# A fused attention and feed-forward kernel: q instead of w_in is loaded in permuted order, and the key-value state is copied across the partition halves

## The chip, the core and the metric

The kernel runs on one core of one Trainium2 chip. The metric is the device time of one execution in microseconds; three runs of the kernel before gave 832.87 in the median (832.84 to 837.14). Five engines work side by side, each through its own instructions in order: TensorE (PE; its weight loads are shown as PEld), VectorE (DVE), ScalarE (ACT), GpSimd (POOL) and SyncE (SP), which here issues nearly all DMAs. The DMAs of a core share 16 DMA engines.

## The reference

Linear attention over 8 batches, 8 heads, 576 tokens, 64 features a head, and then a two-layer feed-forward network on the 4608 rows of 512 that this gives. All numbers are wide: q, k and v are 32-bit floats, the two weight matrices 64-bit floats, which the kernel takes as 64-bit words.

```python
q_s = exp(q - max(q, axis=-1));  q_s = q_s / (sum(q_s, axis=-1) + 1e-9)   # over the 64 features
k_s = exp(k - max(k, axis=2));   k_s = k_s / (sum(k_s, axis=2) + 1e-9)    # over the 576 tokens
kv  = einsum('bhsd,bhse->bhde', k_s, v)                                   # the state: 64 x 64 a head
x   = einsum('bhsd,bhde->bhse', q_s, kv).transpose(0, 2, 1, 3).reshape(4608, 512)
h   = x @ w_in                                                            # 512 x 2048
g   = maximum(h, 0) + log1p(exp(-abs(h)))                                 # softplus
out = g @ w_out                                                           # 2048 x 512
```

## The kernel before

**Tiles.** Two heads make a pair and fill 128 partitions, 64 each; there are 4 pairs (`HP`). The tokens are cut into 9 tiles of 512. The middle dimension of 2048 is cut into 16 weights (`NJ`): weight k holds 128 columns of w_in (as 128 rows of 512 words) and the 128 rows of w_out that go with them.

**State.** For each batch b and pair h, `kv_unit` (L466) takes a tile of keys and values, finds the maxima of the keys, shifts (L516), takes exponentials (L522), multiplies keys and values on TensorE (L527, L532), inverts the sums of the keys (L540, L541) and copies the 64 x 64 state of both heads, scaled, out of PSUM (`keep`, L545) into `kvs[b % 2]`. For b = 0 the maxima come by way of TensorE (L495, L512), which also runs fillers on the identity matrix (L1159).

**q and x.** A q tile holds for 512 tokens the four pairs, 128 partitions x 4 x 512 floats. `q_unit` (L566) takes its softmax: maxima (L576), exchange between neighbouring blocks of 32 partitions (L563), shift (L590), exponential (L593), sums (L596), division (L625), in halves of two pairs. `flip` (L657, for the first tile L680) transposes in blocks of 32. `x_product` (L640, L646) then makes x for two pairs in four quarter products: state and q of one partition half (`zs`), written to one partition half of one of two PSUM banks. The bank is chosen by the partition half z that q and state are read from, and the half of the bank by the pair y within the group of two. So the features of x come out in another order than that of the pairs.

**Where that order is made good.** Before, w_in is loaded with its rows and pieces permuted to that order, by two DMAs of half the partitions each (L286). w_out goes in as it is (L290).

**Weights.** Each weight is turned from 64-bit words into floats and then into a high and a low part: top bits (`top_w`, T, L317), scaling (`scale_w`, M, L309 and L311), sign (`sign_w`, S, L328 and L330), `join_w` (J, L339), and the split into high (P, L350) and low (Q, L352). The first two weights are used unsplit (L708, L758). `up` (U, L720 to L722) and `down` (O, L762 to L764) multiply high x high, low x high and high x low; `softplus` (A, L729) empties the bank of `up`, `split_g` (G, L735 and L738) splits its result. From tile 3 on, two tiles are multiplied together with seven products in place of eight (L847 to L849, L961 to L963), from parts of the weights that were stored to DRAM and are fetched again.

**What sets the order.** The string `ORDER` lists some 3000 steps, and every engine gets its instructions in that order; nothing is reordered later. Around the change it reads `w0.20 b0 b1 q0.0 n k0.0.1 n q0.1 n n ... l0 ... l1 ... l2`: b0 and b1 load the two halves of the first q tile, n loads a tile of keys and values, l a weight, L (as L1) a later q tile by `q_load` (L553). All of these are issued by SP in that order, so a load waits for those ahead of it, and for its buffer. Tiles of keys and values from batch 1 on have two buffers, and GpSimd fills their spare rows (L455) before each load. Weights 10 to 15 are loaded with the tiles of keys and values of batch 1 (`kv_next`, L1044).

Of the kernel before, what the change touches and what calls it, by code (L numbers as in the profile page):

```python
# [15 lines left out]
AF = mybir.ActivationFunctionType  # L16
# [4 lines left out]
B, H, S, D = 8, 8, 576, 64  # L21
DM, DF = 512, 2048
NT = B * S
HP = H // 2
# [13 lines left out]
START = [P * sum(SUBS[:t]) for t in range(len(SUBS) + 1)]  # L38
# [8 lines left out]
TOK = P * max(SUBS)  # L47
# [164 lines left out]
def tile_attn_ffn(  # L212
# [69 lines left out]

    def load_w(k):
        raw[k] = wp.tile([P, 2, DM], I64, name=f"w{k}")
        for y in range(2):
            nc.sync.dma_start(  # L286
                out=raw[k][D * y:D * (y + 1), 0].rearrange("p (g z c) -> p g z c", g=2, z=2),
                in_=w_in[k].rearrange("(z p) (g y c) -> y p g z c", z=2, g=2, y=2)[y],
            )
        nc.sync.dma_start(out=raw[k][:, 1], in_=w_out[k])  # L290

    def words(k, dtype):
# [173 lines left out]
    def kv_unit(b, h, bank):  # L466

        t = loaded.pop((b, h))
        kt, vt = t[:, :, :, 0:D], t[:, :, :, D:KVW if b else 2 * D]
        wide, ps = bank[:, 0:P], (bank[:, 0:D + 1] if b else bank[:, P:P + D])  # L470
        total = ps[:, D:D + 1] if b else banks[h % 2][:, h // 2:h // 2 + 1]
        rest = warm[:, P + D * h:P + D * (h + 1)]
        state = {}

        on_pe = b <= ON_PE

        def top():
            if not b:
                return
            mx = state["mx"] = sm.tile([P, 2, D], F32, name="mx", bufs=3)  # L480
            nc.vector.tensor_reduce(out=mx, in_=kt.rearrange("p c z d -> p z d c"), op=ALU.max, axis=AX.X)  # L481
            if not on_pe:
                mb = state["mb"] = sm.tile([P, 2, D], F32, name="mx", bufs=3)
                nc.gpsimd.partition_all_reduce(  # L484
                    mb.rearrange("p z d -> p (z d)"), mx.rearrange("p z d -> p (z d)"), channels=P,
                    reduce_op=bass_isa.ReduceOp.max,
                )

        def turn():
            if not b:  # L490
                for c in range(NCH, -1, -1):
                    rows = P if c < NCH else TAIL
                    for z in range(2):
                        zs = slice(z * D, (z + 1) * D)
                        nc.tensor.matmul(  # L495
                            bank[zs, c * P:(c + 1) * P] if c < NCH else rest[zs], lhsT=kt[0:rows, c, z],
                            rhs=ident[0:rows, 0:rows], start=True, stop=True,
                        )
                return
            nc.tensor.transpose(wide, state["mx"].rearrange("p z d -> p (z d)"), ident)  # L500

        def across():
            state["m1"] = sm.tile([P, 1], F32, name="m1", bufs=2)
            if not b:
                nc.vector.tensor_reduce(out=state["m1"], in_=rest, op=ALU.max, axis=AX.X)
                nc.vector.tensor_tensor(
                    out=bank[:, 0:1], in0=bank[:, 0:1], in1=state["m1"], op=ALU.max
                )
            nc.vector.tensor_reduce(out=state["m1"], in_=wide if b else bank, op=ALU.max, axis=AX.X)

        def spread():
            nc.tensor.transpose(wide, state["m1"].broadcast_to([P, P]), ident)  # L512

        def shift():
            mb = wide.rearrange("p (z d) -> p z d", z=2) if on_pe else state["mb"]
            nc.vector.tensor_tensor(  # L516
                out=kt, in0=kt, in1=mb.unsqueeze(1).broadcast_to([P, NCH + 1, 2, D]), op=ALU.subtract
            )

        def power():  # L520
            cz = t.rearrange("p c z w -> p (c z) w")[:, :, 0:D]
            nc.scalar.activation(cz, cz, AF.Exp)  # L522

        def product():
            for c in range(0 if b else NCH + 1):
                for z in range(2):
                    nc.tensor.matmul(  # L527
                        total[z * D:(z + 1) * D], lhsT=kt[:, c, z], rhs=one, start=c == 0, stop=c == NCH
                    )
            for c in range(NCH + 1):  # L530
                for z in range(2):
                    nc.tensor.matmul(  # L532
                        ps[z * D:(z + 1) * D], lhsT=kt[:, c, z], rhs=vt[:, c, z], start=c == 0, stop=c == NCH
                    )
            if b == 1:
                kv_next()

        def scale():
            r = sm.tile([P, 1], F32, name="r", bufs=2)
            nc.vector.tensor_scalar(out=r, in0=total, scalar1=EPS, scalar2=W_SCALE, op0=ALU.add, op1=ALU.mult)  # L540
            nc.vector.reciprocal(r, r)  # L541
            state["r"] = r

        def keep():
            nc.scalar.activation(kvs[b % 2][:, h], ps[:, 0:D], AF.Copy, scale=state["r"])  # L545

        none = lambda: None
        return [top] + ([turn, across, spread] if on_pe else [none] * 3) + [shift, power, product, scale, keep]
# [3 lines left out]

    def q_load(t):  # L553
        qt = (wp if t >= SOLO and t % 2 else qp).tile([P, HP * TOK], F32, name="w4" if t >= SOLO and t % 2 else "qt")
        nc.sync.dma_start(out=qt, in_=q[:, HP * START[t]:HP * START[t + 1]])
        qtiles[t] = qt.rearrange("p (h n) -> p h n", h=HP)

    def swapped(m, copy=nc.vector.tensor_copy):

# [497 lines left out]
    with tc.manual_schedule():  # L1057
# [28 lines left out]
        def do(token):  # L1086
# [31 lines left out]
            elif kind == "q":  # L1118
                unit(("q", at[0]), lambda: q_unit(at[0]))[at[1]](*(nc.gpsimd,) * sum(at[2:]))
            elif kind == "x":  # L1120
                t, h, i = at
                unit(("x", t, h), lambda: make_x(t, h))[i]()
            elif kind == "L":
                q_load(at[0])
            elif kind == "D":
                keep_w(at[0])
            elif kind == "R":
                {0: fetch_w, 2: fetch_sums, 3: fetch_in, 4: fetch_in_b}[at[0]](*at[1:])
            elif kind == "Y":
                s, i = at[:2]  # L1130
                unit(("Y", s), lambda: sum_unit(s))[i](*(nc.gpsimd,) * sum(at[2:]))
            elif kind == "y":
                s, i = at[:2]
                unit(("y", s), lambda: sum_out_unit(s))[i](*(nc.gpsimd,) * sum(at[2:]))
            elif kind == "r":
                fetch_block(*at)
            elif kind == "t":
                less_g(*at[:3], *(nc.gpsimd,) * sum(at[3:]))
            elif kind == "e":
                split_right(*at[:4], *(nc.gpsimd,) * sum(at[4:]))  # L1140
            elif kind == "d":
                product_out(*at)
            elif kind == "o":
                unit(("o", at[0]), lambda: end_unit(at[0]))[token.split(".")[1]](*at[1:])
            elif kind == "X":
                p, c, name, *more = token[1:].split(".")
                unit(("X", p, c), lambda: operand_unit(int(p), int(c)))[name](*(nc.gpsimd,) * len(more))
            elif kind == "C":
                p, s, i = at
                unit(("C", p, s), lambda: pair_unit(p, s))[i]()  # L1150
            elif kind == "H":
                split_g(*at[:3], *(nc.gpsimd,) * sum(at[3:]))
            elif kind == "I":
                down(*at)
            elif kind == "F":
                finish(*at)
            elif kind == "w":
                for _ in range(at[1]):
                    nc.tensor.matmul(warm[:, 0:P], lhsT=ident, rhs=ident, start=True, stop=True)  # L1159
            elif kind == "b":  # L1160
                half = slice(2 * at[0], 2 * at[0] + 2)
                nc.sync.dma_start(
                    out=qtiles[0][:, half], in_=q[:, 0:HP * TOK].rearrange("p (h n) -> p h n", h=HP)[:, half]
                )
            elif kind == "n":
                place = dict(engine=nc.vector, queue=nc.scalar) if ahead[0] < HP else {}
                if 2 <= ahead[0] < HP:
                    tag = 2 * ahead[0] - 4 if UNSPLIT < NJ else ahead[0] - 1
                    place |= dict(pool=xp, tag=f"x{tag}", shape=(P, HP * TOK))
                kv_prefetch(**place)  # L1170
            elif kind == "l":
                for k in at:
                    load_w(k)
# [41 lines left out]
```

## Time and profile before

| | |
|---|---|
| median of 3 runs | 832.87 us |
| profiled execution | 832.97 us, span 831.1 us |
| PE busy | 805.5 us (97%), 4312 matmuls |
| PEld busy | 640.8 us (77%) |
| DVE busy | 582.4 us (70%) |
| ACT busy | 484.2 us (58%) |
| POOL busy | 115.1 us (14%) |
| granted TensorE clock, mean | 0.992 of full |
| DMA | 193.72 MB, mean 233 GB/s |
| w_in loads (L286) | 32 of 256 KB, 10.7 us from issue to landing (median) |
| w_out loads (L290) | 16 of 512 KB, 11.6 us |
| q loads | 2 of 512 KB, 4.6 us; 8 of 1024 KB |

Times count from the start of the span. An instruction's row gives its start, how long it took, engine, line, operation, the tile written and the tile read, shapes, and in brackets how long the engine stood idle before it and what ended that. A count (x2) merges neighbours. Matmuls overlap: a row's 0.4 us is longer than the distance to the next. SP's rows are issues, not transfers.

### The profile page before, as it was taken

What the parts mean: (1) busy time and instruction counts of PE and PEld (TensorE: products, weight loads), DVE (VectorE), ACT (ScalarE), POOL (GpSimd) and SP (SyncE); (2) the same over time, 40 slices, a digit from 0 to 9 for tenths busy, and PEclk for the clock granted to TensorE, in tenths of its full rate; (3) what the DMA queues carried; (4) which work ended last, traced back from release to release, by engine and by line L of the source; (5) the groups of instructions that cost most, each with busy time, mean ns of one, the idle gap of its engine ahead of it and who ended that gap; (6) DMA issues with size and microseconds to landing.
All of it is one profiled execution on the core that took longest, in us unless ns stands there. A gap on an engine that the chain in (4) does not pass through costs nothing.

```text
span 831.1 us, 12042 instructions
## 1 busy us (share of the span) xinstructions
PE 805.5 (97%) x4312; PEld 640.8 (77%) x4312; DVE 582.4 (70%) x934; ACT 484.2 (58%) x792; POOL 115.1 (14%) x211
## 2 busy tenths in 40 slices
PE   8898899999999999999999999999999999999997
PEld 7566686888777787788788777888777788888886
DVE  7656895369688886968489889765596852227884
ACT  3687883545554755577786555766574542446652
POOL 1220003101010210101010012250000110700017
PEclk9899999999999999999999999999999999999999
DMA  9999956647689888998696575984766554948845
GB/s 278 247 247 242 246 222 226 206 144 267 233 289 342 273 315 297 323 325 294 227 290 196 164 243 166 314 257 156 226 192 186 183 172 170 271 134 278 253 141 88
DMA packets 120890, 193.72 MB, mean 233 GB/s; under 512 B 8256, under 2 KB 98624, under 8 KB 110592
## 3 DMA queue, kind: packets, MB, share of 16 engines
q1 hardware_dynamic: 117568, 186.67, 70.3%
q0 software_dynamic: 2944, 6.04, 3.6%
q8 instruction: 34, 0.56, 0.3%
q10 hardware_dynamic: 320, 0.26, 0.1%
q14 instruction: 24, 0.20, 0.1%
HBM read 149.95 MB, written 42.99 MB: 232 GB/s over the span
## 4 chain that ended last, share of the span: by engine, by line
PE 81%; DMA 8%; DVE 3%; ACT 2%; POOL 2%; SPq 1%; issue 1%; POOLq 0%; ACTq 0%; DVEq 0%
PE po L847 6%; PE po L849 6%; PE po L848 6%; PE po L963 6%; PE po L961 6%; PE po L962 6%; PE po L762 4%; PE ph L720 4%; PE po L764 4%; PE po L763 4%; PE ph L721 4%; PE ph L722 4%; DMA w<-in_w_in 4%; PE ph L847 3%; PE ph L848 3%; PE ph L849 3%
## 5 line engine op out<-in xcount | busy, mean ns | idle before, releaser
L1006 POOL DMA_DIRECT2D out<-w x92 | 59.4, 653 | 296.9 <-DVE w L998 292.3
L720 PE MATMUL ph<-x,w 128*128 128x512 f32 x164 | 66.3, 404 | 3.5 <-ACT g L729 3.4
L762 PE MATMUL po<-w,g_hi 128*128 128x512 f32 x164 | 65.1, 397 | 2.1 <-ACT g_hi L735 2.1
L721 PE MATMUL ph<-x,w 128*128 128x512 f32 x164 | 64.6, 394 | 0.1
L722 PE MATMUL ph<-x,w 128*128 128x512 f32 x164 | 64.6, 394 | 0.0
L764 PE MATMUL po<-w,g_lo 128*128 128x512 f32 x164 | 64.2, 391 | 0.1
L944 DVE TENSOR_TENSOR g_lo<-w,g_hi 128x512 fp32r<-128x512 f32 x74 | 49.4, 682 | 21.1 <-ACT g_hi L941 21.1
L763 PE MATMUL po<-w,g_hi 128*128 128x512 f32 x164 | 64.0, 390 | 0.0
L941 ACT CAST g_hi<-w 128x512 fp32r<-128x512 f32 x74 | 45.5, 619 | 19.7 <-PE po L962 13.2
L928 DVE TENSOR_TENSOR w<-w,w 128x512 f32<-128x512 f32 x72 | 48.4, 681 | 2.7 <-ACT w L881 1.7
L941 ACT CAST w<-w 128x512 fp32r<-128x512 f32 x52 | 31.8, 620 | 25.7 <-PE po L962 18.9
L870 DVE TENSOR_TENSOR w<-po,w 128x512 f32<-128x512 f32 x24 | 16.5, 686 | 40.8 <-PE po L849 40.8
L738 DVE TENSOR_TENSOR g_lo<-g,g_hi 128x512 fp32r<-128x512 f32 x46 | 31.1, 681 | 19.6 <-ACT g_hi L735 19.5
L729 ACT ACTIVATE g<-ph 128x512 f32<-128x512 f32 x48 | 28.5, 597 | 27.4 <-PE ph L722 27.2
L847 PE MATMUL po<-w,x 128*128 128x512 f32 x112 | 44.3, 395 | 0.0
L849 PE MATMUL po<-w,x 128*128 128x512 f32 x112 | 43.7, 390 | 0.0
L848 PE MATMUL po<-w,x 128*128 128x512 f32 x112 | 43.6, 390 | 0.0
L484 POOL PARTITION_ALL_REDUCE mx<-mx x20 | 20.5, 1027 | 165.8 <-DVE mx L481 145.1
L481 DVE TENSOR_REDUCE mx<-kvt 128x128 f32<-128x640 f32 x28 | 36.8, 1320 | 8.8 <-DMA kvt<-in_kv_tail 6.9
L720 PEld LDWEIGHTS ph<-x,w 128*128 128x128 f32 x164 | 31.2, 190 | 13.1 <-ACT g L729 4.4
L735 ACT CAST g_hi<-g 128x512 fp32r<-128x512 f32 x46 | 28.2, 619 | 21.7 <-PE po L763 15.4
L944 DVE TENSOR_TENSOR w<-w,w 128x512 fp32r<-128x512 f32 x52 | 35.1, 683 | 6.5 <-ACT w L941 6.2
(380 smaller groups left out, 2243.6 us busy)
## 6 DMA issues: line engine op xcount, KB each, us to landing
x<-sums SPq DMA_DIRECT2D x24, 1024.0 KB, 5.6
kvt<-in_kv SPq DMA_DIRECT2D x30, 512.0 KB, 6.8
kept<-w SPq DMA_DIRECT2D x15, 1024.0 KB, 8.2
w<-kept SPq DMA_DIRECT2D x13, 1024.0 KB, 8.3
x<-sums_out SPq DMA_DIRECT2D x44, 256.0 KB, 5.2
w<-kept SPq DMA_DIRECT2D x36, 256.0 KB, 4.6
x<-kept SPq DMA_DIRECT2D x36, 256.0 KB, 4.7
w<-sums_out SPq DMA_DIRECT2D x36, 256.0 KB, 5.7
```

The source lines that it names most:

```text
L720: nc.tensor.matmul(ph, lhsT=w_hi, rhs=x_hi, start=h == 0, stop=False)
L721: nc.tensor.matmul(ph, lhsT=w_lo, rhs=x_hi, start=False, stop=False)
L722: nc.tensor.matmul(ph, lhsT=w_hi, rhs=x_lo, start=False, stop=h == HP - 1)
L762: nc.tensor.matmul(po, lhsT=g_hi[:, ms], rhs=w_hi, start=j == 0, stop=False)
L763: nc.tensor.matmul(po, lhsT=g_hi[:, ms], rhs=w_lo, start=False, stop=False)
L764: nc.tensor.matmul(po, lhsT=g_lo[:, ms], rhs=w_hi, start=False, stop=j == NJ - 1)
L847: nc.tensor.matmul(ph, lhsT=w_hi, rhs=x_hi, start=c == 0 and i in (0, 4), stop=False, **more)
L848: nc.tensor.matmul(ph, lhsT=w_lo, rhs=x_hi, start=False, stop=False, **more)
L849: nc.tensor.matmul(ph, lhsT=w_hi, rhs=x_lo, start=False, stop=c == 1, **more)
L941: nc.scalar.copy(ring[p, i, s][0], right_of(p, i, s))
L944: engine.tensor_tensor(out=lo, in0=right_of(p, i, s), in1=hi.bitcast(F32), op=ALU.subtract)
L1006: nc.gpsimd.dma_start(out=rows(n, c)[:, 32 * a:32 * a + 32].rearrange("(b r) e -> r b e", r=32), in_=flipped(n)[32 * a:32 * a + 32, c].rea ...
```

## The change

The loads of w_in become one DMA of 128 whole rows. A q tile is loaded by four DMAs instead (`q_fetch`): for each group g of two pairs and each partition half z, 64 partitions with 2 pieces of 512 floats. The partition half z of q then holds pair 2g + z, and the pieces y its two heads. The state has to lie the same way, so `keep` copies its two halves separately: head z of pair h goes to the partition half h % 2, place 2 (h // 2) + z. `x_product` stays as it is, and x comes out in the order of the heads.

```diff
     def load_w(k):
         raw[k] = wp.tile([P, 2, DM], I64, name=f"w{k}")
-        for y in range(2):
-            nc.sync.dma_start(
-                out=raw[k][D * y:D * (y + 1), 0].rearrange("p (g z c) -> p g z c", g=2, z=2),
-                in_=w_in[k].rearrange("(z p) (g y c) -> y p g z c", z=2, g=2, y=2)[y],
-            )
+        nc.sync.dma_start(out=raw[k][:, 0], in_=w_in[k])
         nc.sync.dma_start(out=raw[k][:, 1], in_=w_out[k])
...
         def keep():
-            nc.scalar.activation(kvs[b % 2][:, h], ps[:, 0:D], AF.Copy, scale=state["r"])
+            for z in range(2):
+                zs, to = slice(z * D, (z + 1) * D), slice(h % 2 * D, (h % 2 + 1) * D)
+                nc.scalar.activation(kvs[b % 2][to, h // 2 * 2 + z], ps[zs, 0:D], AF.Copy, scale=state["r"][zs])
...
     def q_load(t):
         qt = (wp if t >= SOLO and t % 2 else qp).tile([P, HP * TOK], F32, name="w4" if t >= SOLO and t % 2 else "qt")
-        nc.sync.dma_start(out=qt, in_=q[:, HP * START[t]:HP * START[t + 1]])
         qtiles[t] = qt.rearrange("p (h n) -> p h n", h=HP)
+        q_fetch(t, range(HP // 2))
+
+    def q_fetch(t, groups):
+
+        src = q[:, HP * START[t]:HP * START[t + 1]].rearrange("(y p) (g z n) -> z g p y n", y=2, z=2, g=HP // 2)
+        for g in groups:
+            for z in range(2):
+                nc.sync.dma_start(out=qtiles[t][z * D:(z + 1) * D, 2 * g:2 * g + 2], in_=src[z, g])
...
             elif kind == "b":
-                half = slice(2 * at[0], 2 * at[0] + 2)
-                nc.sync.dma_start(
-                    out=qtiles[0][:, half], in_=q[:, 0:HP * TOK].rearrange("p (h n) -> p h n", h=HP)[:, half]
-                )
+                q_fetch(0, at)
```

## Rows read from the trace of the kernel before

**Rows 1.** The page: share of the span of the chain that ended last, by engine.
```profile
PE 81%; DMA 8%; DVE 3%; ACT 2%; POOL 2%; SPq 1%; issue 1%; POOLq 0%; ACTq 0%; DVEq 0%
```
**Rows 2.** Windows: length, busy us (instructions) of each engine, clock, DMA share, GB/s.
```profile
36.00:100.00 64.00, 57.01 (x280) 39.94 (x279) 43.74 (x59) 52.28 (x62) 9.39 (x15) 0.97 1.05 241
100.00:200.00 100.00, 98.60 (x524) 78.80 (x523) 65.51 (x108) 56.48 (x81) 10.64 (x13) 1.00 0.59 212
```
**Rows 3.** Chain of waits, 0 to 100 us: its shares, and its first transfer.
```profile
by line: DMA w<-in_w_in 32.1%; DMA kvt<-in_kv 20.0%; DMA w<-in_w_out 18.5%; SPq L463 8.3%; SPq L286 2.9%; DVE w L328 2.5%; ACT w L317 1.9%; ACT w L309 1.9%; issue 1.7%; DVE kvt L516 1.5%; ACT L729 1.3%; ACT kvt L522 1.3%; DVE w L339 1.3%; D
...
1.68 6.73 DMA kvt<-in_kv
```
**Rows 4.** Waits of TensorE from 100 us to the end, the longest.
```profile
PE po L762 <- ACT g_hi L735: 2.1, 2, 1.2
```
**Rows 5.** DMA view, stretches 40 to 60, 12 to 14, 632 to 634 us.
```profile
DMA packets 2886, 4.61 MB, mean 230 GB/s; under 512 B 205, under 2 KB 2301, under 8 KB 2872
...
DMA packets 428, 0.44 MB, mean 222 GB/s; under 512 B 27, under 2 KB 417, under 8 KB 428
...
DMA packets 761, 0.74 MB, mean 368 GB/s; under 512 B 43, under 2 KB 761, under 8 KB 761
```
**Rows 6.** Timeline of SP's and VectorE's first work on q.
```profile
0.75 0.88 SPq L1162 DMA_DIRECT2D qt<-in_q  x2
...
4.84 1.22 DVE L576 TENSOR_REDUCE m<-qt 128x32 f32<-128x1024 f32 x1 [1.30 <-DMA qt<-in_q]
```
**Rows 7.** Timeline of VectorE and ScalarE, 20 to 25 us.
```profile
20.57 0.82 DVE L516 TENSOR_TENSOR x<-x,po 128x640 f32<-128x640 f32 x1
...
22.93 1.13 ACT L317 ACTIVATE w<-w 128x1024 uint32<-128x1024 uint8 x1 [3.22 <-DMA w<-in_w_out]
23.96 1.34 ACT L522 ACTIVATE x<-x 128x640 f32<-128x640 f32 x2
```
**Rows 8.** Timeline of TensorE, its first keys and the third tile's product.
```profile
10.12 0.33 PE L495 MATMUL ph<-ident,kvt 64*64 64x64 f32 x4
...
24.73 0.81 PE L527 MATMUL att<-one,x 128*64 128x1 f32 x20 [2.69 <-ACT x L522]
```
**Rows 9.** Windows of 4 us, columns as in rows 2.
```profile
24.00:28.00 4.00, 3.27 (x70) 3.27 (x72) 0.40 (x4) 2.54 (x5) 2.38 (x4) 0.66 1.09 244
...
72.00:76.00 4.00, 3.77 (x9) 2.79 (x10) 3.79 (x5) 3.61 (x6) 0.00 (x0) 0.63 1.08 237
```
**Rows 10.** TensorE's timeline, 72 to 86 us, and two chain rows at full clock.
```profile
72.14 0.49 PE L720 MATMUL ph<-x,w 128*128 128x512 f32 x1 [3.40 <-ACT g L729]
...
76.94 0.39 PE L762 MATMUL po<-w,g_hi 128*128 128x512 f32 x1
...
85.02 0.30 PE L500 MATMUL att<-ident,mx 128*128 128x128 f32 x1 [2.31 <-DVE mx L481]
...
101.94 0.50 PE ph L720
...
104.28 0.23 PE ph L720
```
**Rows 11.** Timeline of VectorE, ScalarE and GpSimd, 64 to 84 us.
```profile
64.36 2.35 DVE L576 TENSOR_REDUCE m<-qt 128x32 f32<-128x1024 f32 x2 [6.38 <-DMA qt<-in_q]
...
67.74 1.23 DVE L339 SCALAR_TENSOR_TENSOR w<-w 128x1024 uint32<-128x1024 uint32 x1
...
83.58 1.29 DVE L481 TENSOR_REDUCE mx<-kvt 128x128 f32<-128x640 f32 x1 [5.89 <-DMA kvt<-in_kv_tail]
...
69.05 1.12 ACT L350 CAST w<-w 128x1024 fp32r<-128x1024 f32 x1 [3.96 <-DVE w L339]
...
65.98 0.20 POOL L455 MEMSET kvt<- 64x128 f32 x1 [3.05 <-ACT w L317]
```
**Rows 12.** The line of the state's copies: instructions, and what ended idle time before them.
```profile
L545 ACT ACTIVATE kvs<-att,r x28: 290/314/356, 50.1 to 568.0; 128x64 f32<-128x64 f32 x28
...
  DVE r L541: 8.0, 5
```
**Rows 13.** VectorE's maxima of q (L576): idle time ended by later q loads.
```profile
  DMA w<-in_q: 2.2, 2
```

## The prediction

> **What bounds the kernel now.** I read the shares of the chain that ended last first: TensorE holds 81% of it, DMA 8%, nothing else over 3% [rows 1]. Whole stretches then tell where that 8% lies: from 100 to 200 us TensorE is idle 1.4 us, from 36 to 100 us it is idle 7.0 us (64 - 57.0), with the DMA engines at 1.05 of their time [rows 2]. The chain of the first 100 us alone is a chain of transfers: 32% of it w_in, 20% keys and values, 18.5% w_out, from 1.68 us on [rows 3]. So the 32 small loads of w_in sit on the path that sets the end, but only until the sixteen weights are in. After 100 us TensorE waits for ScalarE and VectorE alone, 2.1 us at the most for one line [rows 4].
>
> **Why w_in is slow.** A weight is 0.26 + 0.26 MB of w_in (two DMAs, each to 64 partitions, in pieces of 1 KB) and 0.52 MB of w_out (128 partitions, 4 KB pieces). From 40 to 60 us little but weights moves, at 230 GB/s: 1.049 MB / 230 = 4.56 us a weight. Two stretches part the size of the pieces from the height: from 12 to 14 us 390 of 428 packets (417 - 27) are w_in's, and the rate is 222 GB/s; from 632 to 634 us all 718 data packets (761 - 43) are of the same class of size, in transfers to 128 partitions, and the rate is 368 [rows 5]. So the half height costs, not the 1 KB. The Trainium skill, "SBUF — State Buffer", section "Door 1: The DMA port swizzle", has this as a rule: 64 partitions reach 8 of 16 ports, and it measured 196 against 328 GB/s for 1 MiB. By that rule the trace's 222 against 368 is expected; they agree.
>
> **Part 1, w_in whole.** Each of sixteen weights loses one DMA and goes to 128 partitions in 4 KB pieces. At 368 GB/s a weight takes 2.85 us, 1.7 less. Bounds: 0 less (if reading these two tensors is what is slow) and 1.7. SP has 16 issues fewer.
>
> **Part 2, q permuted.** A q tile was one DMA to 128 partitions (the first tile two); it becomes four to 64 partitions in 2 KB pieces. Nearest row: w_in's 222 GB/s, so 4.7 us a tile, 1.9 more than at 368. Bounds: 0 (2 KB pieces make up for it) and 2.9 (half of 368: 5.7 us). The Trainium skill speaks against this part: on the same page, "Can I just issue two DMAs to hit both halves?" says that transfers to the two halves of the partitions serialize (+6% only). By its 196 GB/s a tile would take 5.35 us and everything behind the first would come 0.6 us later than in my sum; w_in's two DMAs are such a pair, and at 222 the trace agrees.
> SP issues three DMAs more per tile, and two more for the first, at 0.44 us (two took 0.88, rows 6): the first key load is issued 0.9 us later, but beside a transfer that is 1.9 us longer, so nothing is added.
>
> **Part 3, up to the first x products (32 us).** What stands behind the first q tile comes 1.9 us later; two weights on the way save 3.4. The wait that decides is ScalarE's 3.22 us for w1, which ends at 22.93; behind it in ScalarE's order are the exponentials of the third and fourth key tile (23.96, 1.34 for both), and TensorE idles 2.69 us until 24.73 for them [rows 7, 8]. New start of that ScalarE work: 22.93 + 1.9 - 3.4 = 21.4. The fourth tile's shift on VectorE ended at 21.39 [rows 7]; VectorE's maxima of q, which waited for q until 4.84 [rows 6], are ahead of it and push it to 23.3 at most. Its exponential began at 24.6, so I take -1.3. The first key tile landed at 8.41 (1.68 + 6.73) and TensorE took it up at 10.12 [rows 3, 8]: there 1.7 of the 1.9 us are covered. Bounds: +1.9 (w1 no earlier) and -4.5: TensorE, idle for less, might keep its clock, which was 0.66 from 24 to 28 us after that idle [rows 9] and stretched the matmuls ahead of the first x product.
>
> **Part 4, 36 to 100 us.**
> (a) 3.4 us before 72.14 [rows 10]. VectorE waits 6.38 us, until 64.36, for the q1 tile, which is queued behind ten weights. The join of w6 (67.74) stands behind the maxima of q1 in its order; ScalarE's split of w6 waits 3.96 us for the join; and the softplus that frees TensorE's bank stands behind that [rows 11]. New landing: 64.36 + 1.9 + 1.9 - 10 x 1.7 = 51.2; VectorE wanted it at 57.98. The gap closes; late next is ScalarE's work on w6 and w7, which it ended at about 65.
> (b) After the gap the clock is 0.63 from 72 to 76 us [rows 9]: twelve matmuls take 4.80 us (72.14 to 76.94) in place of 12 x 0.23 = 2.76 [rows 10]. 2.0 us, gone with the idle.
> (c) 2.3 us before 85.02 [rows 10]: VectorE waits 5.89 us for the fourth key tile of batch 1 [rows 11]. GpSimd's fill of its buffer at 65.98 [rows 11] allows the load; weights 10 to 12 were still in the queue. With q1 in at 51 and three weights at 2.85 they are in by 62, and the tile by about 71 (66.4 and the 4 us that the first q half took from 0.75 to 4.84, rows 6).
> (d) The other 1.3 us are small.
> Together 7.0 + 2.0 = 9.0 us. Not all of it comes back. ScalarE is busy 52.3 of these 64 us [rows 2], TensorE without gaps 55.0; two engines that take turns at nearly equal load hand waits to each other. I give back 2.0 us (bounds 0, and 5.6 if gap (a) alone is won).
>
> **Part 5, the state in two copies.** 32 copies become 64 of half the height and the same width, so 0.31 us each [rows 12]. Two more between 36 and 100 us on a full ScalarE: +0.6. The others are hidden: ScalarE is busy 56 of 100 us after that [rows 2]; uncovered they would be 8 us. The copies do not wait for x products of an earlier batch: what ended ScalarE's idle time before them is VectorE's reciprocal [rows 12].
>
> **Part 6, later q tiles.** VectorE waited for three of them, two of these 2.2 us together [rows 13]. Its first maximum needs half a tile, which lands no later (0.52 MB at 222 is 2.4 us; the whole tile takes 2.85 now); the second comes up to 0.7 us later (1.9 less the 1.2 of the first maximum, rows 6). TensorE waits for no maximum there: 0, bound 3 x 0.7 = 2.1.
>
> **Sum.** -1.3 - 9.0 + 2.0 + 0.6 + 0 = -7.7, against the profiled execution's 832.97 us (831.1 of span and 1.9 around it), which is 0.1 above the median of the runs, 832.87: 825.3. Past 100 us all work moves forward in time together, as TensorE bounds it.
>
> **Rivals.**
> *The clock holds in the opening.* Part 3 at -4.5 and half of the 2.0 kept: -12, 821.0. For it: the idle before 24.73 shrinks to about 1.3 us. Against: ScalarE would need w2 by 24, which lands no earlier than 21.4 + 2.85.
> *ScalarE bounds the opening.* Gap (a) alone is won, part 3 gives 0: 832.97 - 3.4 + 0.6 = 830.2, no change by the bound below. For it: 52.3 us busy of 64. Against: in the same stretch ScalarE itself waits 3.96 us for the join alone.
> *Slower: the weights stay slow*, since the source limits them, while q pays for the half height. Place: the q1 tile, which lands at 64.36 + 3.8, so that the gap before 72.14 grows by 1.9; the opening comes 1.9 later, copies 0.6, later tiles 2.1: +6.5, 839.5. It decides from the point at which a weight takes over 4.2 us (ten weights must save the 3.8 us of two q tiles). For it: half of the bytes in the 230 GB/s is w_out, at full height already. Against: 368 in the same queue at the same size of pieces.
> *The change doesn't do what it says*: the four q loads run at full speed. Then part 3 gains 1.9 more: 823.3, inside the likeliest case's own range.
>
> **How the numbers follow.** Likeliest case 0.58 (own range 821.5 to 828.5), clock holds 0.20, ScalarE bounds 0.14, slower 0.08. The range 819.0 to 831.5 takes in the first three and leaves out the slower case and the tails. About 0.5% (4.2 us) is what a measurement of this kernel can tell from no change: faster 0.78, same 0.14, slower 0.08.
>
> **What would show it.** Right: weights moving at 340 GB/s or more; a DMA share well under 1 before 90 us; no wait of VectorE for q1; no gap of TensorE near 69 and 83 us, and its clock at full there; its matmul of 101.94 us at about 94. Wrong: weights still near 230 GB/s; the first x product (32.06 us) no earlier; new waits of TensorE for ScalarE between 36 and 100 us; a wait for q on TensorE's path after 100 us.

## The result, and the profile after

The kernel after took 824.68 us in the median of 4 runs (823.46 to 826.38), the kernel before 833.19 beside it: a ratio of 0.9889, 95% interval [0.9854, 0.9923]. The forecast was 825.3. The total came out within 0.6 us, but the trace shows that two errors of the forecast's terms, one of 6.3 us and one of 5.2 us, cancelled.

| | before | after |
|---|---|---|
| profiled execution, span | 832.97, 831.1 us | 824.4, 822.6 us |
| PE / DVE / ACT busy | 805.5 / 582.4 / 484.2 us | 801.7 / 584.1 / 497.3 us |
| loads of w_in | 32 of 256 KB, 10.7 us | 16 of 512 KB, 9.2 us |

Lines of after stand 4 further up than those of before from the loads of w_in (L285) to the state's copies (L543), and 5 further down behind the loads of q (L561).

**The lead.** Both kernels run the same 4312 matmuls in the same order. So the start of a matmul in before, less the start of the same matmul in another kernel, says how far that kernel is ahead there. I call it the lead; this table is worked out from the starts in the traces, by the time in before, and the rest of the text reads it:

| us in before | 15 | 32 | 72 | 85 | 112 | 510 | 536 | 560 | 820 |
|---|---|---|---|---|---|---|---|---|---|
| after | -1.9 | 4.3 | 7.9 | 12.5 | 14.0 | 12.5 | 8.2 | 8.2 | 8.8 |
| w_in whole, q as before | 0.5 | 6.2 | 9.8 | 14.3 | 15.9 | 15.9 | 15.9 | 14.4 | 14.6 |
| q permuted, w_in as before | -2.7 | -0.6 | -5.0 | -5.6 | -5.6 | -6.1 | -7.9 | -8.3 | -7.6 |
| state in two copies alone | 0.4 | 0.0 | -2.3 | -3.8 | -4.3 | -4.6 | -4.6 | -4.6 | -4.0 |
| after, w_in in half-height rows | -2.8 | -0.9 | -6.1 | -5.7 | -4.6 | -5.9 | -8.0 | -8.6 | -7.9 |
| after, w_in in 1 KB pieces | -3.1 | 2.7 | 6.3 | 10.9 | 12.4 | 10.9 | 6.7 | 6.7 | 6.6 |
| after, q by four full-height loads | -0.9 | 5.3 | 9.0 | 13.5 | 15.1 | 15.0 | 14.8 | 14.2 | 14.8 |
| after, q laid out ahead | -0.3 | 6.0 | 9.6 | 14.1 | 15.7 | 14.8 | 14.8 | 14.8 | 15.5 |
| after, last q tile behind the sums | -1.5 | 4.7 | 8.3 | 12.9 | 14.4 | 14.1 | 13.7 | 11.6 | 12.3 |

After loses 2 us at first, gains 16 by 112 us, and gives 4.3 back near 520 us. The rows follow that.

A lead compares one execution with one. In the opening it carries a spread of several us: the kernel with the state in two copies is 4.3 us behind at 112 us, although its median is that of before (see the experiments), and 25 runs of before span 831.48 to 839.90 us, with the profiled execution (832.97) near the low end. The step near 520 us is not of that kind. It stands in all four kernels whose q is loaded at half height in the order of after (4.3, 1.8, 2.0 and 4.2 us from 510 to 536 us) and is 0.3 us at the most in the four whose q is loaded at full height.

**The opening.** Windows of after, columns as in [rows 2], which they answer together with [rows 9]:
```profile
24.00:28.00 4.00, 4.00 (x90) 3.81 (x90) 3.86 (x11) 3.48 (x9) 3.26 (x4) 1.00 1.11 327
36.00:100.00 64.00, 64.00 (x330) 48.26 (x329) 54.68 (x72) 62.68 (x78) 8.14 (x15) 1.00 0.82 278
72.00:76.00 4.00, 4.00 (x20) 3.26 (x19) 3.94 (x6) 3.82 (x6) 0.00 (x0) 1.00 0.97 367
80.00:84.00 4.00, 4.00 (x20) 3.06 (x20) 1.69 (x2) 4.00 (x6) 0.00 (x0) 1.00 0.00 0
```
From 36 to 100 us TensorE is never idle (57.0 us busy before), its clock is full, and from 80 to 84 us nothing is left to transfer. ScalarE is busy 62.7 of the 64 us.

The chain of waits of after from 0 to 100 us, its shares by line, answers [rows 3]; almost only TensorE's lines and the first q tile are left in it, w_in and w_out are gone:
```profile
by line: PE ph L725 9.5%; PE ph L726 9.1%; PE ph L727 9.1%; PE po L767 7.7%; PE po L768 7.5%; PE po L769 7.5%; PE po L763 7.4%; PE ph L713 7.1%; DMA qt<-in_q 6.3%; PE ph L1164 4.6%; PE att L528 2.8%; PE po L528 2.5%; PE att L523 2.3%; PE po
```
Transfers of after, DMA view of 12 to 16, 44 to 48 and 504 to 512 us; it answers [rows 5]:
```profile
DMA packets 450, 1.65 MB, mean 412 GB/s; under 512 B 48, under 2 KB 48, under 8 KB 450
...
DMA packets 395, 0.78 MB, mean 196 GB/s; under 512 B 42, under 2 KB 42, under 8 KB 395
...
DMA packets 1087, 2.01 MB, mean 251 GB/s; under 512 B 107, under 2 KB 107, under 8 KB 1087
```
The first is weights alone: 412 GB/s where 230 was the rate before. The second is the q1 tile's four half-height loads, with hardly anything beside them: 196 GB/s. The third is the stretch in which the last two q tiles are loaded, of which more below.

Timeline of VectorE, TensorE and ScalarE in after's opening (it answers [rows 6 to 8] and [rows 11]):
```profile
6.64 1.22 DVE L581 TENSOR_REDUCE m<-qt 128x32 f32<-128x1024 f32 x1 [3.10 <-DMA qt<-in_q]
...
53.55 2.34 DVE L581 TENSOR_REDUCE m<-qt 128x32 f32<-128x1024 f32 x2
...
68.74 1.32 DVE L477 TENSOR_REDUCE mx<-kvt 128x128 f32<-128x640 f32 x1
```
```profile
10.60 0.33 PE L491 MATMUL ph<-ident,kvt 64*64 64x64 f32 x4
...
27.80 2.23 PE L651 MATMUL po<-w,kvs 64*64 64x512 f32 x12
```
```profile
23.36 0.74 ACT L518 ACTIVATE x<-x 128x640 f32<-128x640 f32 x1 [0.63 <-DVE x L512]
```
The first q maximum starts 1.8 us later (4.84 before), the first keys 0.5 later (10.12), the exponential of the fourth key tile 1.2 earlier (24.6), and the first x product 4.3 earlier (32.06). The maxima of q1 and of the fourth key tile of batch 1, for which VectorE had waited 6.4 and 5.9 us, start without a wait.

**Behind the opening.** The longest wait of TensorE from 100 us on (answers [rows 4]), its timeline and windows at the longest, and SP's timeline ahead of it:
```profile
PE ph L852 <- DMA x<-sums: 2.9, 2, 2.7
```
```profile
518.32 0.76 PE L852 MATMUL ph<-x,x 128*128 128x512 f32 x1 [2.68 <-DMA x<-sums]
```
```profile
514.00:518.00 4.00, 1.63 (x8) 1.02 (x6) 4.00 (x5) 0.51 (x1) 0.00 (x0) 0.97 1.03 365
518.00:520.00 2.00, 1.68 (x4) 1.43 (x5) 0.00 (x0) 0.00 (x0) 0.00 (x0) 0.50 1.12 299
520.00:524.00 4.00, 4.00 (x16) 3.22 (x16) 2.14 (x2) 2.73 (x4) 0.70 (x1) 0.85 1.12 326
```
```profile
500.89 2.60 SPq L561 DMA_DIRECT2D w<-in_q  x4
503.54 0.60 SPq L371 DMA_DIRECT2D w<-kept  x1
504.24 2.65 SPq L561 DMA_DIRECT2D qt<-in_q  x4
506.94 0.60 SPq L377 DMA_DIRECT2D spare<-kept  x1
507.64 0.55 SPq L382 DMA_DIRECT2D x<-sums  x1
```
The same steps on SP's timeline of before:
```profile
513.38 0.34 SPq L555 DMA_DIRECT2D w<-in_q  x1
...
514.72 0.34 SPq L555 DMA_DIRECT2D qt<-in_q  x1
...
517.11 0.33 SPq L386 DMA_DIRECT2D x<-sums  x1
```
and, of before and then of after, how long that fetch took from issue to landing (last column; DMA views of the microsecond of its issue):
```profile
x<-sums SPq DMA_DIRECT2D x1, 1024.0 KB, 8.7
```
```profile
x<-sums SPq DMA_DIRECT2D x1, 1024.0 KB, 10.5
```
TensorE's first use of it in before:
```profile
527.97 0.39 PE L847 MATMUL ph<-x,x 128*128 128x512 f32 x1
```
`x<-sums` fetches 1 MB of x that TensorE multiplies at L852. It stands in SP's order behind the last two q tiles. In before it landed at 525.8 (517.11 + 8.7), 2.2 us ahead of its use. In after TensorE wants it 12.3 us earlier (at 518.32 - 2.68 = 515.64), but it is issued only 9.5 us earlier, 2.9 short, and takes 1.8 longer: 2.2 - 2.9 - 1.8 = -2.5, about the 2.7 us of idle. Behind the idle the granted clock is 0.50 of full (1.2 of 2.4 GHz) from 518 to 520 us and 0.85 from 520 to 524, and that turns 2.7 us into 4.3.

### The profile page after: what moved, and what is told of

Same layout as the page of the kernel before. It is cut to its first block, busy times and chain, and to the rows that moved or that the text cites. A ratio compares the mean times of both kernels' runs of the same rounds, so it can differ in the third digit from the quotient of the medians.

```text
span 822.6 us, 12090 instructions
## 1 busy us (share of the span) xinstructions
PE 801.7 (97%) x4312; PEld 637.2 (77%) x4312; DVE 584.1 (71%) x934; ACT 497.3 (60%) x824; POOL 116.0 (14%) x211
## 4 chain that ended last, share of the span: by engine, by line
PE 82%; DMA 6%; DVE 5%; ACT 3%; POOL 2%; issue 2%; SPq 1%; POOLq 0%; ACTq 0%; DVEq 0%
PE po L852 6%; PE po L968 6%; PE po L853 5%; PE po L854 5%; PE po L966 5%; PE po L967 5%; PE ph L725 4%; PE ph L726 4%; PE po L767 4%; PE ph L727 4%; PE po L769 4%; PE po L768 4%; PE ph L852 3%; PE ph L854 3%; PE ph L853 3%; PE ph L966 3%
## 5 line engine op out<-in xcount | busy, mean ns | idle before, releaser
L725 PE MATMUL ph<-x,w 128*128 128x512 f32 x164 | 65.5, 400 | 0.0
L726 PE MATMUL ph<-x,w 128*128 128x512 f32 x164 | 64.0, 390 | 0.0
L727 PE MATMUL ph<-x,w 128*128 128x512 f32 x164 | 63.9, 390 | 0.0
L852 PE MATMUL po<-w,x 128*128 128x512 f32 x112 | 44.3, 396 | 0.0
L734 ACT ACTIVATE g<-ph 128x512 f32<-128x512 f32 x48 | 28.4, 598 | 24.9 <-PE ph L727 24.6
L767 PEld LDWEIGHTS po<-w,g_hi 128*128 128x128 f32 x164 | 30.8, 188 | 11.4 <-ACT g_hi L740 3.9
L740 ACT CAST g_hi<-g 128x512 fp32r<-128x512 f32 x46 | 28.2, 620 | 18.3 <-PE po L768 13.5
```

The source lines that it names most:

```text
L725: nc.tensor.matmul(ph, lhsT=w_hi, rhs=x_hi, start=h == 0, stop=False)
L726: nc.tensor.matmul(ph, lhsT=w_lo, rhs=x_hi, start=False, stop=False)
L727: nc.tensor.matmul(ph, lhsT=w_hi, rhs=x_lo, start=False, stop=h == HP - 1)
L767: nc.tensor.matmul(po, lhsT=g_hi[:, ms], rhs=w_hi, start=j == 0, stop=False)
L852: nc.tensor.matmul(ph, lhsT=w_hi, rhs=x_hi, start=c == 0 and i in (0, 4), stop=False, **more)
```

## The experiments

| kernel | median us (runs) | ratio to before, 95% interval |
|---|---|---|
| after | 824.68 (4) | 0.9889 [0.9854, 0.9923] |
| w_in whole, q as before | 818.44 (4) | 0.9800 [0.9758, 0.9843] |
| q permuted, w_in as before | 841.91 (10) | 1.0080 [1.0050, 1.0110] |
| state in two copies alone | 835.96 (10) | 1.0007 [0.9981, 1.0032] |
| before with ten fillers | 838.54 (10) | 1.0025 [0.9995, 1.0054] |
| after, w_in in half-height rows | 843.23 (4) | 1.0121 [1.0078, 1.0164] |
| after, w_in in 1 KB pieces | 824.26 (4) | 0.9882 [0.9850, 0.9914] |
| after, q by four full-height loads | 818.67 (4) | 0.9825 [0.9803, 0.9847] |
| after, q laid out ahead | 817.98 (4) | 0.9824 [0.9797, 0.9850] |
| after, last q tile behind the sums | 821.99 (4) | 0.9847 [0.9803, 0.9892] |

The median of before beside the second to fifth rows was 836.03 (25 runs), beside the sixth to ninth 833.15, beside the last 834.56 (7 runs each): kernels of different groups compare by the ratio.

**w_in whole, and nothing else.**
```diff
-        for y in range(2):
-            nc.sync.dma_start(
-                out=raw[k][D * y:D * (y + 1), 0].rearrange("p (g z c) -> p g z c", g=2, z=2),
-                in_=w_in[k].rearrange("(z p) (g y c) -> y p g z c", z=2, g=2, y=2)[y],
-            )
+        nc.sync.dma_start(out=raw[k][:, 0], in_=w_in[k])
```


> Only w_in changes: one DMA of 128 whole rows; q's loads and the state's copy stay as before (x then comes out in an order that does not fit w_in). Theory (the half height of the loads costs): the opening gains at least the 14.0 us that TensorE's matmuls were ahead in the changed kernel at 112 us, about 15, since the first q tile is not slowed; and nothing of the 5 us that the changed kernel lost again later. 833.2 - 15 = 818, 816 to 820. Rival A (the later loss comes from running ahead of fixed work and not from the q loads): the loss comes here too, 823. Rival B (the permuted q is what sped up the opening): 833.

0.9800: a gain of 2.0%, where after gains 1.1%. Its lead is 15.9 us at 112 us and still 15.9 at 536; the loss near 520 us does not exist in it. It loses 1.4 us near 556 us, where TensorE waits 1.1 us for ScalarE.

**q permuted and the state copied across, with w_in as before.** The rest of the change, `q_fetch` and `keep` as in the diff of the change.

> Only q changes (four half-height DMAs a tile, the state in two copies); w_in is still loaded by two half-height DMAs (x then comes out in an order that does not fit w_in). Theory: the first q tile costs about 2 us in the opening, the second about 2 more by the gap before 72 us, the last two tiles about 4 us near 515 us: 838 to 842. Rival B (the permuted q is what sped up the opening): under 830. Rival C (q at half height is hidden everywhere): 833 to 834.

1.0080: slower alone. The waits of TensorE over the whole run show where:
```profile
PE ph L729 <- ACT g L738: 7.0, 1, 7.0
PE att L500 <- DVE mx L481: 3.4, 1, 3.4
```
These are the two gaps of before in the opening (3.40 and 2.31, [rows 10]), grown to 7.0 and 3.4. The weights and the keys stand behind a q tile that takes longer here, but how much of the growth comes from that is not shown: in the profiled execution of the next kernel, whose loads are those of before, the gaps are 5.6 and 3.5 us, and VectorE waits 8.6 us for the q1 tile, where before it waited 6.4. TensorE's longest wait there:
```profile
PE ph L722 <- ACT g L731: 5.6, 1, 5.6
```
That q permuted costs time rests on the medians. At the end the lead of one part is +14.6 and of the other -7.6, together 7.0; the change as a whole has 8.8. By the ratios, 2.0% gained and 0.8% lost make 1.2, and the change has 1.1. The parts about add up.

**The state in two copies, to the same place.**
```diff
-            nc.scalar.activation(kvs[b % 2][:, h], ps[:, 0:D], AF.Copy, scale=state["r"])
+            for z in range(2):
+                zs = slice(z * D, (z + 1) * D)
+                nc.scalar.activation(kvs[b % 2][zs, h], ps[zs, 0:D], AF.Copy, scale=state["r"][zs])
```


> The kernel before with the state copied in two halves to where it was before; the result is the same. Theory: 32 more ScalarE copies of 0.3 us, of which four lie before 80 us on a full ScalarE: 833.2 + 0 to 1.0. Rival (the copies are on the path everywhere): + 8 to 10, 842.

1.0007 [0.9981, 1.0032]: no cost that can be measured in the medians; the lag of its one profiled execution goes with VectorE's longer wait for the q1 tile, 8.6 us for 6.4. In after a half-height copy takes what a whole one took, 308 ns against 315 (ScalarE's groups by line, after and then before), so 32 more of them are 10 us of busy time, and by the medians they are covered:
```profile
L543 ACT ACTIVATE kvs<-att,r 64x64 f32<-64x64 f32 x56 | 17.3, 308 | 8.5 <-DVE r L537 7.8
```
```profile
L545 ACT ACTIVATE kvs<-att,r 128x64 f32<-128x64 f32 x28 | 8.7, 315 | 8.0 <-DVE r L541 8.0
```

**Height or pieces of w_in.** Two kernels change after's load of w_in: the first loads whole 4 KB rows to 64 partitions twice, the second 1 KB pieces to 128 partitions twice.
```diff
-        nc.sync.dma_start(out=raw[k][:, 0], in_=w_in[k])
+        for y in range(2):
+            nc.sync.dma_start(out=raw[k][D * y:D * (y + 1), 0], in_=w_in[k][D * y:D * (y + 1)])
```


> The kernel after, but each weight's w_in is loaded by two DMAs to 64 partitions each, in whole 4 KB rows. Theory (half height is what made w_in slow): weights move at about 230 GB/s again from 40 to 60 us where no q tile is moving, and the time goes back to that of q alone permuted, 838 to 842 us. Rival (the 1 KB pieces of the permuted w_in were slow): as after, 823 to 826 us.

```diff
-        nc.sync.dma_start(out=raw[k][:, 0], in_=w_in[k])
+        for g in range(2):
+            nc.sync.dma_start(
+                out=raw[k][:, 0, 256 * g:256 * g + 256].rearrange("p (z c) -> p z c", z=2),
+                in_=w_in[k].rearrange("p (z g c) -> g p z c", z=2, g=2)[g],
+            )
```


> The kernel after, but each weight's w_in is loaded by two DMAs to 128 partitions each in 1 KB pieces. Changed: the order of w_in's 1 KB pieces within a row. Theory (half height is what made w_in slow): weights move at 340 GB/s or more and the time is as after, 823 to 827 us. Rival (the 1 KB pieces were slow): about 230 GB/s, 835 us or more.

1.0121 and 0.9882: it is the height. The first kernel's 843.23 us is 1.2 above its forecast; the second's is inside. The DMA views of the stretches where weights move, 44 to 48 us of the half-height kernel and 12 to 16 us of the other:
```profile
DMA packets 279, 0.96 MB, mean 241 GB/s; under 512 B 44, under 2 KB 44, under 8 KB 279
```
```profile
DMA packets 826, 1.55 MB, mean 388 GB/s; under 512 B 63, under 2 KB 575, under 8 KB 826
```
Whole 4 KB rows to half the partitions move at 241 GB/s, although half of a weight's bytes are w_out's at full height. All partitions with a third of the bytes in 1 KB pieces (512 packets of 575 - 63) move at 388, against after's 412 in 4 KB rows. So these pieces cost 6% of the rate (11% by [rows 5], 368 GB/s with all in 1 KB pieces), and half height for half of the bytes 42%. From 40 to 60 us, with the half-height q1 tile in the stretch, the second kernel's mean is 299 GB/s and after's 316.

**Why the later loss: the height of the q loads, or their number?** The same four loads a tile, each of one pair to all 128 partitions:
```diff
-        for g in groups:
-            for z in range(2):
-                nc.sync.dma_start(out=qtiles[t][z * D:(z + 1) * D, 2 * g:2 * g + 2], in_=src[z, g])
+        src = q[:, HP * START[t]:HP * START[t + 1]].rearrange("p (h n) -> p h n", h=HP)
+        for h in (2 * g + z for g in groups for z in range(2)):
+            nc.sync.dma_start(out=qtiles[t][:, h], in_=src[:, h])
```


> The kernel after, but the four loads of a q tile each fetch one pair to all 128 partitions (2 KB pieces, 256 KB each, as many loads and bytes as after). Left out: the permutation of q, so the x products read q in another order than the state's. It tells the half height of the q loads from their number. Theory (half height): q tiles land at the full rate, the sums behind q tiles 7 and 8 land early enough, TensorE's 2.7 us wait near 518 us and the clock drop behind it go, and the lead over the kernel before stays flat from 112 us on: 817 to 820 us. Rival A (it is the number of loads that SP issues, 0.65 us each there): loss near 518 us still about 4, 823 to 825 us. In the opening both expect a lead of about 15 at 112 us, 1 more than after's 14.0.

0.9825, and the loss is gone: the lead is 15.0 at 510 us and 14.8 at 536. TensorE's one wait for a fetch of sums is short, and it is for the next fetch, at 523.22 us:
```profile
PE po L852 <- DMA x<-sums: 0.3, 1, 0.3
```
SP still issues four loads for each of the two tiles:
```profile
498.36 1.76 SPq L561 DMA_DIRECT2D w<-in_q  x4
...
500.79 2.48 SPq L561 DMA_DIRECT2D qt<-in_q  x4
...
504.16 0.72 SPq L382 DMA_DIRECT2D x<-sums  x1
```
They take 4.2 us where after's take 5.3 and before's two single loads 0.7. How long the fetch took in this kernel, and when TensorE first used it:
```profile
x<-sums SPq DMA_DIRECT2D x1, 1024.0 KB, 8.8
```
```profile
513.11 0.47 PE L852 MATMUL ph<-x,x 128*128 128x512 f32 x1
```
It landed at 513.0 (504.16 + 8.8), 0.1 us ahead of its use. So the rival is right about a part: of the 2.2 us of slack in before, the number of loads eats 2.1. But that alone makes no idle. The half height adds the rest: another 0.8 us until the issue (2.9 - 2.1) and 1.8 us in the queue. The rate in 504 to 512 us, 251 GB/s in after, is here
```profile
DMA packets 1728, 2.95 MB, mean 368 GB/s; under 512 B 112, under 2 KB 942, under 8 KB 1601
```

**q laid out in the new order in memory**, so that a tile is one full-height load again (the first tile two); the state is still copied across and w_in is whole. The matching edit of `q_fetch` is left out of this listing.
```diff
-        [qa[:, :, :, a // 32:e // 32].reshape(P, -1) for a, e in zip(START, START[1:])], axis=1
+        [qa[:, :, :, a // 32:e // 32].reshape(2, D, HP // 2, 2, e - a).transpose(3, 1, 2, 0, 4).reshape(P, -1)
+         for a, e in zip(START, START[1:])], axis=1
...
```


> The kernel after, but q arrives in memory already in the permuted order, so a q tile is again one load to 128 partitions (the first tile two). w_in is whole, the state is copied across. This has what the change wins and not what it pays. Theory: the opening as with w_in alone whole (lead 15 to 16 us at 112 us), no wait near 518 us, state copies 0 to 0.6: 818 to 819.5 us. Rival (the loss near 518 us comes from the copies of the state or from the changed order of x, not from the q loads): 822 to 825 us.

0.9824, 817.98 us: faster than both kernels, and level with w_in whole alone. It keeps what the change wins and drops what it pays. The rival (copies or the order of x cause the later loss) falls: the lead is 14.8 at 510 us and 14.8 at 560. It moves work out of the kernel, into the layout of its input, and is a fair version only where that layout can be chosen.

**The remedy in the order.** The last q tile's load (L8) and first maximum (q8.0) behind the fetch of the sums (R2.10):
```diff
-... C1.1.4 L8 o0.flip.2.1 C1.1.10 C1.1.5 q7.4 q8.0 R4.1.1 C1.2.7 R2.10 n ... C1.2.2 q8.1 R3.3.1 n
+... C1.1.4 o0.flip.2.1 C1.1.10 C1.1.5 q7.4 R4.1.1 C1.2.7 R2.10 L8 n ... C1.2.2 q8.0 q8.1 R3.3.1 n
```


> The kernel after with two steps of ORDER moved: the four loads of the last q tile (L8) and the first maxima on it (q8.0) stand behind the step R2.10, which fetches the sums of x, in place of ahead of it. Nothing is left out. Theory (the sums land late because two half-height q tiles are queued ahead of them): the fetch of the sums is issued about 2.6 us earlier and has one half-height tile ahead of it, so the wait near 518 us shrinks to under 1 us, the clock holds behind it, and 3 to 4.3 of the 4.3 us lost there come back: 820.4 to 822 us. Rival (the sums are late for another reason, such as the writes of the sums themselves or a late VectorE): the lead still falls by about 4 near 520 us, 824 to 825.5 us. What speaks against the theory's gain: the last q tile now comes later, and its softmax with it.

0.9847, 821.99 us, inside the forecast, but not quite by its way. The wait near 518 us is not shortened, it is gone (the lead is 14.1 at 510 us, 13.7 at 536). The next fetch of sums is late in its place, behind the moved q tile and two tiles of keys and values (TensorE's timeline):
```profile
525.81 0.47 PE L851 MATMUL po<-x,x 128*128 128x512 f32 x1 [1.81 <-DMA x<-sums]
```
The lead falls to 11.6 by 560 us. So of 4.3 us lost, 2.5 are lost still, a little later: the delay has moved to the next fetch in the queue.

**What the idle ahead of the first x product costs.** Ten fillers more on TensorE (20 matmuls in the trace), ahead of the product of the third key tile of before:
```diff
-    q0.8 k0.3.3 q0.12 w1.6 q0.13 k0.2.5 ...
+    q0.8 k0.3.3 q0.12 w1.6 q0.13 w2.10 k0.2.5 ...
```


> The kernel before with ten more filler matmuls on TensorE ahead of the third key tile's product, so that it does not stand idle for the whole 2.7 us before 24.73 us; no transfer changes. Theory (the clock is a part of the opening's gain, apart from the transfers): the clock stays near full from 24 to 32 us (0.66 and 0.50 before), the first x product comes at 29.5 to 30.5 us in place of 32.06, and the end 1 to 2.5 us earlier: 831 to 832. Rival (the transfers alone made the first x product 4.3 us earlier): the first x product within 0.5 us of 32.06 and 833.

The two halves of that expectation part. The windows of this kernel and then of before at 28 to 32 us:
```profile
28.00:32.00 4.00, 3.92 (x27) 2.27 (x30) 3.66 (x7) 2.65 (x6) 0.00 (x0) 1.00 1.10 261
```
```profile
28.00:32.00 4.00, 4.00 (x30) 3.71 (x27) 3.93 (x10) 1.59 (x3) 0.00 (x0) 0.50 1.14 251
```
```profile
29.60 3.09 PE L646 MATMUL po<-w,kvs 64*64 64x512 f32 x16
24.58 1.36 ACT L522 ACTIVATE x<-x 128x640 f32<-128x640 f32 x2
```
With the idle filled the clock is full, and the first x product (third row, the filler kernel's) starts at 29.60, 2.5 us ahead of 32.06, with no transfer any earlier. The exponentials of the third and fourth key tile (last row) start 0.6 us later than before's 23.96, so from them on the full clock is worth 3.1 us. But the end is not earlier (1.0025): the transfers behind it are as late as before, and from 36 to 100 us TensorE is idle for 9.0 us (55.0 busy) where before it was 7.0. An earlier start was worth nothing here without earlier weights.

## Why the prediction was right, and where it was not

By the lead, the terms of the sum came out so:

| term | forecast | measured |
|---|---|---|
| Part 3, to the first x product | -1.3 | -4.3 |
| Parts 4 and 5, 32 to 112 us | -7.0 + 0.6 | -9.7 |
| Part 6 and all behind | 0 (bound 2.1) | +5.2 |
| sum | -7.7 | -8.8 |

The spans differ by 8.5.

**What bounds, and Part 1: right.** It was the loads of w_in, until the weights are in, and the half height, not the 1 KB: shown by the two kernels that part them. The size was too small: weights move at 412 GB/s, not 368, so 2.55 us each (1.049 MB / 412) for the forecast's 2.85.

**Part 2: right, and priced a little low.** The q1 tile moved at 196 GB/s, not at w_in's 222, so a tile takes 5.35 us (1.049 MB / 196) for 4.7. The Trainium skill, "SBUF — State Buffer", section "Door 1: The DMA port swizzle", gives 196 GB/s for 64 partitions at 1 MiB; the trace agrees. The first maximum of q starts 1.8 us later, near the 1.9 by which the forecast moved what stands behind the first tile. Against the kernel with four full-height loads it costs after about 1 us at the first x product and at 112 us (leads of 5.3 and 4.3, 15.1 and 14.0), and against q laid out ahead 1.7.

**Part 3: the work moved as worked out, and the clock was left out of it.** The forecast put the exponential of the fourth key tile 1.3 us earlier; it is 1.2 earlier. The step that failed is "I take -1.3": it set the first x product equal to that exponential and kept the clock's loss whole, as a bound and a rival with a chance of 0.20. The idle ahead of it went from 2.69 us to none (TensorE is busy 4.00 of the 4 us from 24 to 28), and the clock is 1.00 from 24 to 28 us where it was 0.66. The filler kernel shows the clock's part by itself: 3.1 us from the exponentials on, and with the 1.2 they come earlier that is the 4.3. The argument against it, that ScalarE would need w2 by 24 us, failed too. These rows of ScalarE in after show why:
```profile
22.01 0.72 ACT L518 ACTIVATE x<-x 128x640 f32<-128x640 f32 x1
27.40 1.16 ACT L313 ACTIVATE w<-w 128x1024 uint32<-128x1024 uint8 x1
```
The exponential of the third key tile starts at 22.01 (23.96 before), and the last work of TensorE ahead of its product (L608) at 23.32, 1.6 us later than before (L603, 21.73); so the idle closes from both sides. ScalarE takes up w2 only at 27.40.

**Part 4: the gaps right, the give-back wrong.** All three named terms went: no wait for q1, the clock full from 72 to 76 us, no wait for the fourth key tile. Nothing was given back. "Two engines that take turns at nearly equal load hand waits to each other" did not hold: ScalarE is full, 62.7 of 64 us, and TensorE has no idle time at all. The matmul of 101.94 us, forecast at about 94, started at 88.1. That a second engine is nearly full is not a price until a row shows who waits.

**Part 5: too small to be seen.** Forecast 0.6; the kernel with the copies alone gives 1.0007 with an interval of 0.25% to either side, so not even the direction is shown.

**Part 6: wrong, and beyond its bound.** It looked at the readers of the q tiles alone, VectorE's maxima. For these it held: their waits for later q tiles grow from 2.2 to 4.5 us and none reaches TensorE. It left out what stands behind the q tiles in SP's queue, the fetch of the sums, although the forecast counted just that in the opening (weights behind the first and second tile). The trace of before would have given it: the fetch had 2.2 us of slack, three issues more for each of two tiles at 0.44 us are 2.6, and each tile was priced at 1.9 us more in the queue, beside work that comes forward by 7.7. Instead the part was closed with "TensorE waits for no maximum there: 0".

So the total was right by luck: 6.3 us of gain that the forecast left out met 5.2 us of loss that it left out (sizes from single executions). Of the rivals, "the clock holds" was nearest in the opening (a gain of 12, measured 14.0), and "weights stay slow" was farthest.

What stays open: after also loses 0.9 us near 262 us and 0.6 near 365 us. The kernel with q laid out ahead loses 0.8 at the first place as well, and two of the others lose nothing at either; no run parts these from the spread between executions.

## What to carry to other kernels

In this kernel the slow transfers were paid for by what stands behind them in the queue, not by their readers; for every load that a change slows, list the next loads on the same queue and when each is needed, in the whole run and not in the opening alone. A load that must be permuted is better permuted on the side where it can stay at all 128 partitions: here 1 KB pieces cost 6 to 11% of the rate (388 and 368 for 412 GB/s) and half the partitions about half of it (196). When a change takes an idle time of TensorE away, price the matmuls behind it at the full clock too.

## What the runs showed of the hardware that was not expected

- A mix of equal bytes to 64 and to 128 partitions, all in 4 KB rows, moved at 241 GB/s. One after the other, at the 196 of half-height q loads and the 412 of full-height rows, they would make 266 (2 / (1/196 + 1/412)): half-height loads saved no time beside full-height ones in the queue.
- An issue of a half-height q load took SP 0.65 us (2.60 for four), a full-height one of the same bytes 0.44 to 0.62 (1.76 and 2.48 for four), a whole tile in one load 0.34.
- ScalarE took 308 ns for a copy of 64 partitions and 315 for one of 128 at the same width: half the partitions save nothing.
